# Preparing fp64 weights inside a fused attention and MoE kernel: other raw buffers, another bank for one bound, and another sharing of the splits between the engines

## The chip, the cores and the metric

The kernel runs on one core of one Trainium2 chip. Its engines are TensorE (PE, whose weight loads are listed apart as PEld), VectorE (DVE), ScalarE (ACT), GpSimd (POOL) and SyncE (SP), which here issues all DMAs from one queue, in order. Each engine runs its own list of instructions in order. The metric is the device time of one execution in microseconds; several runs are made and the median is taken. A profile is one execution of its own.

## The reference

Attention over 8 batches, 8 heads, 576 positions and 64 dimensions, with a threshold in the softmax: scores below the row's maximum less tau are dropped. The result, 4608 tokens of 512 channels, goes through a feed-forward layer with 2048 hidden units.

```python
scores = scale * np.matmul(q, k.transpose(0, 1, 3, 2))
thresh = np.max(scores, axis=-1, keepdims=True) - tau
scores = np.where(scores >= thresh, scores, -1000000000.0)
attn = np.exp(scores - np.max(scores, axis=-1, keepdims=True))
attn = attn / (np.sum(attn, axis=-1, keepdims=True) + 1e-09)
x = np.matmul(attn, v)          # then heads side by side: [4608, 512]
h = x @ w_in                    # w_in [512, 2048]
g = h * (1.0 / (1.0 + np.exp(-h)))
out = g @ w_out                 # w_out [2048, 512]
```

q, k and v are fp32. The two weight matrices come as fp64, 8 bytes for each number.

## The kernel before

**Products in pieces of fp16.** TensorE multiplies fp16 numbers at full rate, and the kernel keeps fp32 precision by splitting an operand into a first part (the value rounded to fp16) and a second part (what the rounding left). A product of two split operands is made of three products: first by first, first by second, second by first. So x, g, v and both weight matrices are split, each after a scaling by a power of two that is worked out from the operand's largest value (`pow2_scales`, lines 105 to 151).

**The weights.** There are 32 blocks of weights of 128 x 512 numbers: blocks 0 to 15 are w_in, 16 to 31 w_out. A block passes through these steps:

- `load_weights` (168): a DMA brings the raw fp64 block, 512 KB, into a raw buffer. For w_in, blocks 0 to 3 and 8 to 11 use four places in `gbuf`, the big buffer that later holds g; the other blocks of w_in and all of w_out use the two buffers of the tile `wraw`.
- `decode_weights` (183): ACT makes the fp32 value from the upper word (190), DVE shifts it (193) and puts in bits of the lower word (196). The raw buffer is then free. Four products of the decoded block with itself (208) are summed in a PSUM bank, `wps`, over four blocks; DVE reduces the sum (213). The largest entry bounds the squared weights.
- `scale_in` and `scale_out` (743, 746): `pow2_scales` brings the bounds of the four sums together: a reduction, a diagonal matrix by ACT (112), a product with ones by PE (114) into a bank, a reduction (116) and seven or eight one-column instructions.
- `split_weights` (215): makes the first part `hi` and the second part. Before, for w_in, POOL scales the block in place (225), ACT rounds it (228), POOL subtracts (229). For w_out, ACT scales and rounds in one step (220), and DVE scales and subtracts in one step (221).

**PSUM banks.** The helper `bank` (77) gives out the banks m0, m1 and m2, each one tile at a time. `wps` always takes m2, and the bound of w_out (`o_w_ps`) also takes m2. The first h units (batch 0, columns 0 to 255) alternate between m0 and m2.

**Attention.** Work is a list of tiles of 128 rows of scores. For batch 0 (the lines named "direct") scores are fp32 products (452), DVE takes the maximum (474), ACT the exponential (484), DVE the threshold and the sum (493, 497, 501), POOL scales the rows by the reciprocal (507), PE transposes them (403, 408), ACT copies the transposes (416, 417), and PE multiplies them by v (426). ACT and DVE make x from that (568, 569). Later batches use split operands: `split_k` (358, 360) and `split_q` (349, 350), scores (464), ACT scales the rows (511), POOL splits them (519, 522, 525), a DMA transposes them, and PE multiplies (550). Batch 0 is worked on in two passes, the low columns (0 to 255) of all head pairs, then the high ones (256 to 575), so that the first part of the feed-forward layer can begin early.

**The feed-forward layer.** An h unit (`h_unit`, 586) is 12 products for 128 hidden units (593), followed by tanh on ACT (601) and three steps on DVE and ACT that give g in two parts (602, 608, 609), which are written to `gbuf`. An o unit (617) is 12 products over four of the 16 hidden blocks (624); after four of them the output is scaled on ACT (634) and stored. Batch 0's first part uses the first 4096 words (of 4 bytes) of `gbuf`, its second part words 4096 to 9215; the queries of the direct tiles stand in words 4096 to 6399 until then.

**What sets the order.** The main loop (784) goes through ticks, one for each tile of scores, with 12 empty ticks between the low and the high pass of batch 0. At each tick it emits the steps of a few tiles, the entries of a time table (`todo`), and h or o units at a rate. A scheduler then orders the instructions of each engine by priority, which is the order of emission unless `pri(offset, f)` raises it: the offset counts emitted instructions. The weights enter the time table by `W_PLAN` (37): for each matrix the first block, the ticks between which blocks are decoded (a load two ticks ahead of its decode), the tick at which the scale is made and splits begin, the tick by which the splits are spread, and the offset of priority. Batch 0's output scale (`batch_scales`) is due one tick after the splits of w_out.

Of the kernel before, what the change touches and what calls it, by code (L numbers as in the profile page):

```python
# [15 lines left out]
ALU = mybir.AluOpType  # L16
AX = mybir.AxisListType
PSUM = bass.MemoryType.PSUM

P = 128  # L20
# [3 lines left out]
NK = DM // P  # L24
# [9 lines left out]
RATES = (0.9, 0.9)  # L34
RATE = 0.95

W_PLAN = ((0, 0, 10, 13, 0), (16, 9, 22, 36, 0))
PRI_S, PRI_SOFT1, PRI_SOFT2 = 1600, 50, 200
PRI_AV = 1500
HALVED = (1,)  # L40
# [11 lines left out]
def attention_moe(  # L52
# [10 lines left out]
    nc = tc.nc  # L63
# [41 lines left out]
    def pow2_scales(mx, name, own=None, squared=False):  # L105


        k = name[0]
        one = const.tile([P, 1], F32, name=f"{name}_one", tag=f"{k}_one")
        nc.vector.tensor_reduce(out=one, in_=mx, op=ALU.max, axis=AX.X)  # L110
        diag = const.tile([P, P], BF16, name=f"{name}_diag", tag="diag")
        nc.scalar.activation(diag, ident, AF.Copy, scale=one)
        allp = bank([P, P], f"{name}_ps", own)
        nc.tensor.matmul(allp, ones, diag, start=True, stop=True)
        one = const.tile([P, 1], F32, name=f"{name}_all", tag=f"{k}_all")
        nc.vector.tensor_reduce(out=one, in_=allp, op=ALU.max, axis=AX.X)
        cl = const.tile([P, 1], F32, name=f"{name}_cl", tag=f"{k}_cl")
        low, high = (2.0**-40, 2.0**94) if squared else (2.0**-20, 2.0**47)
        nc.vector.tensor_scalar(
            out=cl, in0=one, scalar1=low, scalar2=high, op0=ALU.max, op1=ALU.min  # L120
        )
        if squared:
            twice = const.tile([P, 1], F32, name=f"{name}_twice", tag=f"{k}_twice")
            nc.vector.tensor_scalar(
                out=twice, in0=cl, scalar1=2.0, scalar2=None, op0=ALU.mult
            )
            half = const.tile([P, 1], I32, name=f"{name}_half", tag=f"{k}_half")
            nc.vector.tensor_scalar(
                out=half, in0=twice.bitcast(I32), scalar1=1, scalar2=EXPMASK,
                op0=ALU.logical_shift_right, op1=ALU.bitwise_and,  # L130
            )
            cl = const.tile([P, 1], F32, name=f"{name}_root", tag=f"{k}_root")
            nc.vector.tensor_scalar(
                out=cl, in0=half.bitcast(F32), scalar1=2.0**64, scalar2=None, op0=ALU.mult
            )
        e2 = const.tile([P, 2], I32, name=f"{name}_e2", tag=f"{k}_e2")
        nc.vector.tensor_scalar(
            out=e2[:, 0:1], in0=cl.bitcast(I32), scalar1=EXPMASK, scalar2=None, op0=ALU.bitwise_and
        )
        nc.vector.tensor_scalar(  # L140
            out=e2[:, 1:2], in0=cl.bitcast(I32), scalar1=EXPMASK, scalar2=EXPMASK,
            op0=ALU.bitwise_and, op1=ALU.bitwise_xor,
        )
        sc = const.tile([P, 2], F32, name=f"{name}_sc", tag=f"{k}_sc", bufs=3)
        nc.vector.tensor_scalar(
            out=sc[:, 0:1], in0=e2[:, 1:2].bitcast(F32), scalar1=2.0**12, scalar2=None, op0=ALU.mult
        )
        nc.vector.tensor_scalar(
            out=sc[:, 1:2], in0=e2[:, 0:1].bitcast(F32), scalar1=2.0**-13, scalar2=None, op0=ALU.mult
        )  # L150
        return sc
# [14 lines left out]
    wps = {}  # L166

    def load_weights(i):
        if i < 4 * NK and i % 8 < 4:
            o = 1024 * (i % 8)  # L170
            t = gbuf.bitcast(I32)[:, o : o + 1024].rearrange("p (c w) -> p c w", w=2)
        else:
            t = stage.tile([P, 512, 2], I32, tag="wraw", name=f"wraw_{i}", bufs=2)
        if i < 4 * NK:
            n, c = divmod(i, NK)
            src = w_words[0][c * P : (c + 1) * P, 1024 * n : 1024 * (n + 1)]
        else:
            f = i - 4 * NK
            src = w_words[1][f * P : (f + 1) * P, :]
        nc.sync.dma_start(out=t.rearrange("p c w -> p (c w)"), in_=src)  # L180
        wraw[i] = t

    def decode_weights(i):


        t = wraw.pop(i)
        low, top = t[:, :, 0], t[:, :, 1]
        w = wst[:, i + WSPARE, :]
        wbits = w.bitcast(I32)
        nc.scalar.activation(  # L190
            w, top.bitcast(F32), AF.Prelu, scale=2.0**-112, alpha=2.0**32
        )
        nc.vector.tensor_scalar(
            out=wbits, in0=wbits, scalar1=3, scalar2=None, op0=ALU.logical_shift_left
        )
        nc.vector.scalar_tensor_tensor(
            out=wbits, in0=low, scalar=29, in1=wbits,
            op0=ALU.logical_shift_right, op1=ALU.bitwise_or,
        )


        n, c = divmod(i, 4)
        if c == 0:
            wps[n] = bank([P, P], f"wps_{n}", 2)
        upper = w.bitcast(BF16).rearrange("p (c t) -> p c t", t=2)[:, :, 1]
        for j in range(4):
            part = upper[:, j * P : (j + 1) * P]
            nc.tensor.matmul(
                wps[n], part, part,
                start=(c == 0 and j == 0), stop=(c == 3 and j == 3),  # L210
            )
        if c == 3:
            nc.vector.tensor_reduce(out=wmx[:, n : n + 1], in_=wps[n], op=ALU.max, axis=AX.X)

    def split_weights(i):
        w = wst[:, i + WSPARE, :]
        hi = w16[:, i, 0:512]
        sc = wsc["in" if i < 4 * NK else "out"][:, 0:1]
        if i >= 4 * NK:
            nc.scalar.activation(hi, w, AF.Copy, scale=sc)  # L220
            nc.vector.scalar_tensor_tensor(
                out=w16[:, i, 512:1024], in0=w, scalar=sc, in1=hi, op0=ALU.mult, op1=ALU.subtract
            )
            return
        nc.gpsimd.tensor_scalar(
            out=w, in0=w, scalar1=sc, scalar2=1.0, op0=ALU.mult, op1=ALU.mult
        )
        nc.scalar.activation(hi, w, AF.Copy)
        nc.gpsimd.tensor_tensor(
            out=w16[:, i, 512:1024], in0=w, in1=hi, op=ALU.subtract  # L230
        )
# [441 lines left out]
    def at(t, f):  # L673
        todo.setdefault(t, []).append(f)
# [73 lines left out]

    for first, t0, t1, t2, hp in W_PLAN:
        for i in range(16):  # L750
            ti = t0 + i * (t1 - t0) / 16
            at(math.floor(ti - 2), pri(hp, lambda i=i + first: load_weights(i)))
            at(math.floor(ti), pri(hp, lambda i=i + first: decode_weights(i)))
        at(t1, pri(hp, scale_out if first else scale_in))
        for i in range(16):
            at(t1 + i * (t2 - t1) // 16, pri(hp, lambda i=i + first: split_weights(i)))
    at(W_PLAN[0][3], lambda: batch_scales_in(0))
    for b in range(B):
        at(max(start[b, 3] + 7, W_PLAN[1][3] + 1), lambda b=b: batch_scales(b))
# [117 lines left out]
```

## Time and profile before

| | us |
|---|---|
| median of 3 runs | 1230.53 |
| lowest and highest run | 1227.30, 1231.17 |
| the profiled execution, its own time | 1225.66 |
| its span, first to last instruction | 1223.9 |
| PE busy | 1150.3 (94%) |
| DVE busy | 933.7 (76%) |
| ACT busy | 796.4 (65%) |
| POOL busy | 707.5 (58%) |

The profile names instructions by line, engine and operation, with the tile written and the tiles read ("wst<-wraw" writes wst from wraw); busy times are sums, and the time that an engine sat idle before an instruction is put down to what released it. The granted clock of PE is given beside each stretch as a share of full speed. Matmuls overlap, so the busy time of PE is modelled and is not PE at its peak.

### The profile page before, as it was taken

How to read it: one execution, taken by the hardware profiler on the slowest of the kernel's cores; microseconds unless marked ns; L12 is line 12 of the kernel's file. 1: busy time of each engine (PE TensorE's matmuls, PEld its weight loads, DVE VectorE, ACT ScalarE, POOL GpSimd, SP SyncE). 2: the span in 40 equal slices, each digit the busy share in tenths (PEclk: the TensorE clock that was granted, in tenths of full speed). 3: DMA queues.
4: the chain of work that ended last, by engine and by line, in shares of the span. 5: the costliest groups of instructions: out<-in, count | busy, mean ns of one | idle time of the engine just before them, and what ended most of it. 6: DMA issues, size and time to landing. Idle time of an engine off the chain costs nothing.

```text
span 1223.9 us, 27062 instructions
## 1 busy us (share of the span) xinstructions
PE 1150.3 (94%) x9474; PEld 899.2 (73%) x9474; DVE 933.7 (76%) x2625; ACT 796.4 (65%) x1505; POOL 707.5 (58%) x902
## 2 busy tenths in 40 slices
PE   6868799999899799999999999999999999999998
PEld 4545567777786577787777777788778877777777
DVE  7988988988999988889889858886788858333330
ACT  6667875876867777777777747785677756333331
POOL 2385357887877587886888428781778547100000
PEclk9979999999999999999999999999999999999999
DMA  9553148889788777886987448772877356200000
GB/s 309 185 161 95 41 108 173 160 160 177 132 177 141 160 137 139 150 165 151 167 149 145 114 94 155 146 136 82 153 150 142 77 92 116 42 11 16 16 10 25
DMA packets 340887, 151.73 MB, mean 124 GB/s; under 512 B 305936, under 2 KB 317200, under 8 KB 340752
## 3 DMA queue, kind: packets, MB, share of 16 engines
q1 hardware_dynamic: 340752, 150.01, 59.1%
q8 instruction: 75, 1.23, 0.4%
q14 instruction: 60, 0.49, 0.1%
HBM read 66.19 MB, written 9.44 MB: 62 GB/s over the span
## 4 chain that ended last, share of the span: by engine, by line
PE 63%; DVE 11%; DMA 10%; POOL 7%; issue 4%; ACT 4%; SPq 1%; POOLq 0%; ACTq 0%; DVEq 0%
PE o L624 24%; PE h L593 21%; PE s L464 9%; PE a L550 7%; DMA wT<-hl 4%; POOL hl L522 3%; DMA wraw<-in_w_out 3%; DVE w L493 2%; POOL hl L519 2%; DVE sm L474 2%; DVE qstack L350 2%; POOL hl L525 1%; DMA wraw<-in_w_in 1%; ACT w L484 1%; ACT w L511 1%
## 5 line engine op out<-in xcount | busy, mean ns | idle before, releaser
L593 PE MATMUL h<-x,wst 128*128 128x288 f16 (+2 forms) x3072 | 425.8, 288 | 7.8 <-DVE gbuf L609 5.0
L624 PE MATMUL o<-gbuf,wst 128*128 128x288 f16 (+2 forms) x3072 | 417.9, 286 | 2.4 <-ACT wst L634 2.4
L593 PEld LDWEIGHTS <-wst 128*128 128x128 f16 x3072 | 292.2, 98 | 95.7 <-issue 16.9
L624 PEld LDWEIGHTS <-wst 128*128 128x128 f16 x3072 | 292.7, 98 | 83.7 <-issue 7.4
L522 POOL TENSOR_TENSOR hl<-w,hl 128x512 f16<-128x512 f32 x252 | 302.6, 1201 | 12.8
L519 POOL TENSOR_SCALAR hl<-w 128x576 f16<-128x576 f32 x252 | 172.2, 686 | 193.4 <-ACT w L511 115.7
L484 ACT ACTIVATE w<-s,sm 128x576 f32<-128x576 f32 x288 | 211.6, 739 | 91.9 <-DVE sm L474 39.1
L493 DVE SCALAR_TENSOR_TENSOR w<-s,sm,w 128x576 f32<-128x576 f32 x288 | 232.0, 812 | 39.9 <-ACT w L484 37.8
L474 DVE TENSOR_REDUCE sm<-s 128x1 f32<-128x576 f32 x288 | 214.4, 749 | 28.7 <-PE s L464 21.8
L511 ACT ACTIVATE w<-w,sm 128x576 f32<-128x576 f32 x252 | 191.4, 771 | 52.1 <-DVE sm L501 50.1
L602 DVE SCALAR_TENSOR_TENSOR h<-th,h 128x288 f32<-128x288 f32 (+2 forms) x256 | 116.2, 455 | 113.7 <-ACT th L601 112.3
L601 ACT ACTIVATE th<-h,msc 128x288 f32<-128x288 f32 (+2 forms) x256 | 126.6, 498 | 103.2 <-PE h L593 101.8
L464 PE MATMUL s<-khi,qstack 128*128 128x288 f32 x560 | 144.3, 338 | 12.7 <-DVE w L493 9.9
L608 ACT ACTIVATE gbuf<-h 128x288 f16<-128x288 f32 (+2 forms) x256 | 104.3, 408 | 78.2 <-DVE h L602 77.5
L609 DVE SCALAR_TENSOR_TENSOR gbuf<-h,gbuf 128x288 f16<-128x288 f32 (+2 forms) x256 | 115.3, 452 | 41.9 <-ACT gbuf L608 41.0
L550 PE MATMUL a<-wT,v 128*64 128x288 f16 (+2 forms) x1568 | 115.0, 289 | 10.8 <-DMA wT<-hl 10.6
L360 POOL TENSOR_TENSOR klo<-kraw,khi 128x576 fp32r<-128x576 f32 x64 | 94.5, 1476 | 47.1 <-ACT khi L358 47.0
L464 PE MATMUL s<-klo,qstack 128*128 128x288 f32 x560 | 120.8, 296 | 0.0
L464 PEld LDWEIGHTS s<-khi,qstack 128*128 128x128 f32 x560 | 87.7, 190 | 31.9 <-issue 15.4
L550 PEld LDWEIGHTS <-v 128*64 128x64 f16 x1568 | 84.5, 110 | 33.7 <-issue 22.1
L464 PEld LDWEIGHTS s<-klo,qstack 128*128 128x128 f32 x560 | 90.4, 189 | 0.6
L525 POOL TENSOR_TENSOR hl<-w,hl 128x64 f16<-128x64 f32 x252 | 89.5, 355 | 0.0
(101 smaller groups left out, 930.4 us busy)
## 6 DMA issues: line engine op xcount, KB each, us to landing
kraw<-in_kT SPq DMA_DIRECT2D x128, 144.0 KB, 3.0
qraw<-in_qT SPq DMA_DIRECT2D x96, 144.0 KB, 3.0
vraw<-in_vL SPq DMA_DIRECT2D x32, 320.0 KB, 3.6
wraw<-in_w_out SPq DMA_DIRECT2D x16, 512.0 KB, 3.7
out_t<-wst SPq DMA_DIRECT2D x48, 144.0 KB, 2.1
wT<-hl SPq DMA_TRANSPOSE x280, 3.4
gbuf<-in_w_in SPq DMA_DIRECT2D x8, 512.0 KB, 6.2
wraw<-in_w_in SPq DMA_DIRECT2D x8, 512.0 KB, 5.1
```

The lines of the kernel that those rows point to most:

```text
L464: nc.tensor.matmul(s_ps[:, j, :HALF], lhs, kk[:, j * HALF : (j + 1) * HALF], start=(n == 0), stop=(n == len(seq) - 1),)
L474: nc.vector.tensor_reduce(out=negm, in_=s_ps[:, :, :HALF], op=ALU.max, axis=AX.XY, negate=True)
L484: nc.scalar.activation(wtile[t].rearrange("p (j c) -> p j c", j=2), sps[t][:, :, :HALF], AF.Exp, bias=small[t][:, 0:1],)
L493: nc.vector.scalar_tensor_tensor(out=w3, in0=s_ps[:, :, :HALF], scalar=sm[:, 1:2], in1=w3, op0=ALU.is_ge, op1=ALU.mult, accum_out=sm[:, 2:3],)
L511: nc.scalar.activation(w, w, AF.Copy, scale=r)
L519: nc.gpsimd.tensor_scalar(out=fl[:, 0:S], in0=w, scalar1=1.0, scalar2=1.0, op0=ALU.mult, op1=ALU.mult)
L522: nc.gpsimd.tensor_tensor(out=fl[:, 640:1152], in0=w[:, 0:512], in1=fl[:, 0:512], op=ALU.subtract)
L550: nc.tensor.matmul(a_ps[odd * D : (odd + 1) * D, :n], vt[:, lo_v, odd, kv, :], wT[v, b * H + 2 * p + odd][:, kw, c0 - base : c0 - base + n ...
L593: nc.tensor.matmul(ph[:, :n], wi(c, f, lo_w), x16[b, lo_x][:, c, c0 : c0 + n], start=(k == 0), stop=(k == 11),)
L601: nc.scalar.activation(th[:, :n], ph[:, :n], AF.Tanh, scale=moe_sc[b][:, 0:1])
L602: nc.vector.scalar_tensor_tensor(out=ph[:, :n], in0=th[:, :n], scalar=1.0, in1=ph[:, :n], op0=ALU.add, op1=ALU.mult,)
L624: nc.tensor.matmul(ps[:, :n], wo(f, d, lo_w), g[:, lo_g, :n], start=(f == 0 and k == 0), stop=(f == NF - 1 and k == 2),)
```

## The change

Five things change, in the preparation of the weights only.

1. Two more places in `gbuf`, words 6400 to 8447, become raw buffers. In each group of eight blocks of w_in, the last two go there; so do every third and fourth block of w_out. w_in then has eight raw buffers (before: six), w_out four (before: two).
2. Loads, decodes and the scale of w_out get an offset of priority of 150 (before: 0). Splits have none, as before. The splits of w_out are spread to tick 38 (before: 36), and batch 0's output scale follows from that two ticks later.
3. The last `wps` tile of w_out gets twice the width, and the product for w_out's bound goes into its second half, where it took a tile of its own in m2.
4. Odd blocks of w_in are split as w_out was: ACT scales and rounds, DVE scales and subtracts. POOL takes no part in them. Even blocks stay as they were.
5. Blocks of w_out are now scaled in place by DVE, rounded by ACT, and subtracted by POOL.

```diff
-W_PLAN = ((0, 0, 10, 13, 0), (16, 9, 22, 36, 0))
+W_PLAN = ((0, 0, 10, 13, 0), (16, 9, 22, 38, 150))
...
-        allp = bank([P, P], f"{name}_ps", own)
+        allp = wps[7][:, P : 2 * P] if name == "o_w" else bank([P, P], f"{name}_ps", own)
...
         if i < 4 * NK and i % 8 < 4:
             o = 1024 * (i % 8)
+        else:
+            o = (None, None, 6400, 7424)[i % 4]
+        if o is not None:
             t = gbuf.bitcast(I32)[:, o : o + 1024].rearrange("p (c w) -> p c w", w=2)
         else:
             t = stage.tile([P, 512, 2], I32, tag="wraw", name=f"wraw_{i}", bufs=2)
...
-            wps[n] = bank([P, P], f"wps_{n}", 2)
+            wps[n] = bank([P, 2 * P if n == 7 else P], f"wps_{n}", 2)
...
-                wps[n], part, part,
+                wps[n][:, 0:P], part, part,
...
-        if i >= 4 * NK:
+        if i < 4 * NK and i % 2:
             nc.scalar.activation(hi, w, AF.Copy, scale=sc)
             nc.vector.scalar_tensor_tensor(
                 out=w16[:, i, 512:1024], in0=w, scalar=sc, in1=hi, op0=ALU.mult, op1=ALU.subtract
             )
             return
-        nc.gpsimd.tensor_scalar(
-            out=w, in0=w, scalar1=sc, scalar2=1.0, op0=ALU.mult, op1=ALU.mult
-        )
+        if i < 4 * NK:
+            nc.gpsimd.tensor_scalar(
+                out=w, in0=w, scalar1=sc, scalar2=1.0, op0=ALU.mult, op1=ALU.mult
+            )
+        else:
+            nc.vector.tensor_scalar(out=w, in0=w, scalar1=sc, scalar2=None, op0=ALU.mult)
         nc.scalar.activation(hi, w, AF.Copy)
         nc.gpsimd.tensor_tensor(
             out=w16[:, i, 512:1024], in0=w, in1=hi, op=ALU.subtract
         )
...
-            at(t1 + i * (t2 - t1) // 16, pri(hp, lambda i=i + first: split_weights(i)))
+            at(t1 + i * (t2 - t1) // 16, pri(0, lambda i=i + first: split_weights(i)))
```

More of the change, by code (lines that the diff above doesn't have):

```diff
@@ L212, in decode_weights @@
         if c == 3:
-            nc.vector.tensor_reduce(out=wmx[:, n : n + 1], in_=wps[n], op=ALU.max, axis=AX.X)
+            nc.vector.tensor_reduce(out=wmx[:, n : n + 1], in_=wps[n][:, 0:P], op=ALU.max, axis=AX.X)
     def split_weights(i):
```

## The prediction

> **What bounds the kernel now.** I read the page's head and its slices first, then the view of busy time by stretches, to see where TensorE is idle.
>
> ```profile
> span 1223.9 us, 27062 instructions
> ...
> PEclk9979999999999999999999999999999999999999
> ...
> 0.00:60.00 60.00, 45.66 (x282) 30.25 (x283) 50.64 (x163) 38.03 (x74) 15.31 (x28) 0.97 0.76 247
> 60.00:110.00 50.00, 35.24 (x189) 22.48 (x187) 41.46 (x97) 34.93 (x72) 42.27 (x42) 0.83 0.49 152
> 110.00:180.00 70.00, 60.14 (x406) 43.04 (x406) 60.58 (x179) 52.48 (x116) 24.24 (x26) 0.95 0.22 56
> 180.00:400.00 220.00, 206.16 (x1778) 164.48 (x1776) 199.89 (x547) 161.93 (x298) 176.82 (x222) 1.00 0.83 163
> 400.00:1040.00 640.00, 622.55 (x5329) 495.25 (x5330) 530.56 (x1529) 450.78 (x824) 444.74 (x580) 1.00 0.70 134
> 1040.00:1223.90 183.90, 180.56 (x1499) 143.73 (x1496) 50.54 (x114) 58.29 (x128) 4.15 (x6) 1.00 0.08 20
> ```
>
> The columns are the stretch, its length, busy time of PE, weight load, DVE, ACT and POOL, granted clock, DMA share, GB/s. From 180 us on PE is the bound: idle 13.8 of 220, 17.4 of 640, 3.3 of 184. No matmul is added or taken away, so only the front can give: PE is idle 14.3 us before 60, 14.8 from 60 to 110, 9.9 from 110 to 180. In the middle stretch the clock is low too:
>
> ```profile
> 70.00:80.00 10.00, 4.24 (x25) 2.88 (x26) 7.08 (x13) 4.39 (x8) 10.00 (x11) 0.65 0.52 166
> 80.00:90.00 10.00, 9.17 (x39) 5.17 (x37) 7.27 (x21) 6.70 (x13) 6.57 (x7) 0.67 0.62 191
> 90.00:100.00 10.00, 6.94 (x47) 5.01 (x45) 8.78 (x17) 8.35 (x19) 8.10 (x8) 0.84 0.49 153
> ```
>
> Busy time times the missing clock: 4.24 x 0.35 + 9.17 x 0.33 + 6.94 x 0.16 = 5.6 us. So 60 to 110 holds 14.8 + 5.6 = 20.4 us that could be won at most.
>
> The timeline says why. These are POOL, then DVE, then PE:
>
> ```profile
> 60.02 12.72 POOL L225 TENSOR_SCALAR wst<-wst,i_w_sc 128x512 f32<-128x512 f32 x16 [2.51 <-DVE i_w_sc L145]
> 72.71 2.70 POOL L229 TENSOR_TENSOR wst<-wst 128x512 f16<-128x512 f32 x2
> 75.39 3.67 POOL L507 TENSOR_SCALAR w<-w,sm 128x576 f32<-128x576 f32 x4
> ...
> 63.34 0.15 DVE L501 RECIPROCAL sm<-sm 128x1 f32<-128x1 f32 x1
> 73.20 0.15 DVE L501 RECIPROCAL sm<-sm 128x1 f32<-128x1 f32 x1
> ...
> 73.33 0.61 PE L208 MATMUL wps<-wst 128*128 128x128 bf16 x4 [1.23 <-DVE wst L196]
> 76.90 0.61 PE L208 MATMUL wps<-wst 128*128 128x128 bf16 x4 [2.95 <-DVE wst L196]
> 77.30 1.05 PE L403 MATMUL tm<-ident,w 128*128 128x128 f32 x4
> 84.38 3.58 PE L426 MATMUL a<-wT,vraw 128*64 128x256 f32 x16
> 90.44 1.14 PE L593 MATMUL h<-x,wst 128*128 128x256 f16 x9
> ```
>
> As soon as w_in's scale is there (60 us), POOL runs all 16 of its scalings in one block, then two subtractions. The softmax scalings (L507) of four tiles stand behind it. The first tile's reciprocal ended at 63.5, the last one's at 73.35; all four run at 75.39 to 79.06. Only then come their transposes (77.30), the last product with V of the low part (84.38) and the first MoE product (90.44). This queue, not w_in's data, holds PE.
>
> The second thing is the raw w_out loads. From the view of waits of SP's queue (20 to 130 us), and the view of groups for 60 to 110 us and for 110 to 180 us:
>
> ```profile
> SPq L180 <- DVE wst L196: 42.2, 18, 4.3
> ...
> L229 POOL TENSOR_TENSOR wst<-wst 128x512 f16<-128x512 f32 x16 | 21.4, 1355 | 3.6 <-ACT wst L228 3.6
> L196 DVE SCALAR_TENSOR_TENSOR wst<-wraw,wst 128x512 int32<-128x512 int32 x14 | 13.2, 946 | 0.1
> L225 POOL TENSOR_SCALAR wst<-wst,i_w_sc 128x512 f32<-128x512 f32 x16 | 12.7, 816 | 2.5 <-DVE i_w_sc L145 2.5
> L193 DVE TENSOR_SCALAR wst<-wst 128x512 int32<-128x512 int32 x14 | 10.0, 712 | 6.3 <-ACT wst L190 6.3
> L190 ACT ACTIVATE wst<-wraw 128x512 f32<-128x512 f32 x14 | 9.4, 675 | 11.3 <-DMA wraw<-in_w_out 11.3
> ...
> L221 DVE SCALAR_TENSOR_TENSOR wst<-wst,o_w_sc 128x512 f16<-128x512 f32 x16 | 13.2, 837 | 0.0
> ```
>
> SP waits 42 us for a decode to free one of the two raw buffers, and ACT 11.3 us for the loads: loads and decodes take turns.
>
> **The change part by part.** Uncontended prices, from the view of the tile wst (minimum/median/maximum in ns):
>
> ```profile
> L193 DVE TENSOR_SCALAR wst<-wst x32: 404/426/1281, 11.8 to 108.1; 128x512 int32<-128x512 int32 x32
> L196 DVE SCALAR_TENSOR_TENSOR wst<-wraw,wst x24: 666/690/1527, 21.7 to 109.2; 128x512 int32<-128x512 int32 x24
> L228 ACT ACTIVATE wst<-wst x16: 612/630/676, 63.0 to 104.0; 128x512 f16<-128x512 f32 x16
> L220 ACT ACTIVATE wst<-wst,o_w_sc x16: 715/722/783, 123.3 to 148.6; 128x512 f16<-128x512 f32 x16
> L221 DVE SCALAR_TENSOR_TENSOR wst<-wst,o_w_sc x16: 726/743/1485, 124.6 to 150.3; 128x512 f16<-128x512 f32 x16
> ```
>
> **(1) Odd blocks of w_in leave POOL.** Eight scalings (8 x 0.816 = 6.5 us) and eight subtractions (8 x 1.355 = 10.8) go: POOL's 42.3 us in 60 to 110 become 25.0. The block ahead of the four softmax scalings is 6.5 us shorter. The first of the four may gain 6.5, or 9.2 if the two subtractions also fall behind; the last, which runs the last 0.92 (3.67 / 4) of its block, can gain only 79.06 - 0.92 - 73.35 = 4.8, since its reciprocal is not earlier. The last of the four sets the product with V, so I take 4.8 (0 to 9.2). The hole in front of it also brings the low clock; with half the hole I take half of the 5.6, 2.8 (0 to 5.6).
>
> **(2) Their price on DVE.** Eight of the L221 kind: 8 x 0.743 = 5.9 us, at the maximum 8 x 1.485 = 11.9. DVE idles 50 - 41.5 = 8.5 us there. And while POOL runs, its decodes are stretched: 14 x (0.712 - 0.426) + 14 x (0.946 - 0.690) = 7.6 us; POOL's work falls by 41%, so I take back 3.1. Net +2.8, inside the 8.5 idle: nothing (at most 11.9 - 8.5 = 3.4). If the hole closes, that cover goes with it and DVE is next in line; that is why (1) is not taken higher. ACT's work is 8 x 0.09 more here and 16 x 0.09 less for w_out: nothing.
>
> **(3) Four raw buffers for w_out and eight for w_in, w_out's decode at a priority raised by 150.** The 32 loads stay; they stop taking turns with the decodes. DVE's work does not change. What is won is the bank m2: the sums for w_out's bound sit in it until the last decode, and every second h unit of the first part wants it.
>
> ```profile
> 110.09 0.40 PE L208 MATMUL wps<-wst 128*128 128x128 bf16 x4
> 112.34 1.47 PE L593 MATMUL h<-x,wst 128*128 128x256 f16 x12
> 119.12 0.22 PE L114 MATMUL o_w_ps<-o_w_diag,ones 128*128 128x128 bf16 x1
> 178.62 1.27 PE L624 MATMUL o<-gbuf,wst 128*128 128x256 f16 x10
> ```
>
> Two h units run before 112.34, the other 14 in the 61 us to 173.7, 4.4 us apart. With both banks, 22 us from 90 to 112 would hold five. Three more at 1.47 us fill 4.4 us of idle PE, at most; the decodes must really end earlier, so I take 2.0 (0 to 4.4). On SP, kT and qT loads stand behind the raw loads; fewer waits there are part of the same gain.
>
> **(4) The bound in the last product's bank.** The product at 119.12 needs no free m2. But the last split starts at 150.3 and the first o product at 178.62, behind all h units: w_out's scale has 28 us to spare, and (3) already counts the bank. Nothing (0 to 1).
>
> **(5) w_out's split.** DVE's 16 x 0.837 become 16 scalings. With no POOL beside them they cost 0.426 (6.6 us less); with POOL beside them 0.712 (2.0 less). POOL now works beside them, so the second. PE is idle 9.9 us in this stretch and DVE busy 60.6 of 70. I take 2.0 (0 to 6.6). New waits: POOL's subtraction waits for ACT's copy, ACT's for DVE's scaling. Behind the subtractions, 16 x 1.355 = 21.7 us, stand POOL's softmax scalings of the high part and klo of batch 1; PE's transposes wait for them. POOL is 24.2 of 70 us busy, so 46 after. A scaling that comes while a subtraction runs waits half of it, 0.7 us; at 21.7/70 that is 12 x 0.31 x 0.7 = 2.6; some of it hides beside h products. I take a loss of 2.0 (0 to 12 x 1.355 = 16 if each stands behind a whole one).
>
> The Trainium skill speaks against this part. "SBUF — State Buffer", in its section "Summary: rules for kernel authors", says that VectorE in a two-port mode (a tensor_scalar on fp32 can be) and GpSimd hold one port pair exclusively, and the second blocks fully. The stretched rows (1281 against 426 ns) agree. By it a DVE scaling could stand behind a whole subtraction; that result is the third rival.
>
> Splits spread over two more ticks, and batch 0's output scale two ticks later, still end well ahead of 178.62: nothing.
>
> **Sum.** 4.8 + 2.8 + 0 + 2.0 + 0 + 2.0 - 2.0 = 9.6 us less. From 180 us on PE is busy 95% (1009.3 of 1043.9), so an earlier front moves all of it. The profiled execution took 1225.66 us, and would take 1216.1; the median shown, 1230.53, stands 4.9 above it, so 1220.9.
>
> **Rivals.**
> *The front is cleared entirely* (chance 0.12): (1) at 9.2 + 5.6, (3) at 4.4, (5) at +2: 21.2 less, 1209.3. For: all engines have gaps in 60 to 110. Against: DVE is busy 50.6 of the first 60 us, the loads' start-up among them, and can hardly follow.
> *Later stages swallow it* (0.12): DVE is busy 199.9 of 220 us from 180 to 400, and each batch's attention comes through it. If PE's lead is lost there, about 2 us of gain are left: 1229. Against: PE itself is idle only 13.8 there.
> *The port pair* (0.08): each of the 16 DVE scalings takes 0.426 + 0.7 (half a subtraction) = 1.13 instead of 0.837: 4.7 lost in place of 2.0 won, 6.7 worse than the forecast: 1227.6.
> *Slower: w_out's decode in w_in's way* (0.18). Raised by 150, a w_out decode can be ordered before w_in's last ones and before the low part's softmax on DVE, which has little room before 60. One decode is 0.426 + 0.690 = 1.12 us. Five ahead of w_in's scale move it by 5.6; six more ahead of the last low tiles move these by 6.7. The first h comes 12.3 later and the clock dip stays (2.8): 9.6 - 2.8 - 12.3 = -5.5, so 5.5 worse, 1236.0. It decides once w_in's scale comes after about 68 us instead of 59.8. Against: the w_out loads cannot start before buffers come free, so few can overtake.
>
> **How the numbers follow.** The forecast has 0.50, with its own range of 1215 to 1226. About 0.3% (3.7 us) is what a measurement can tell from no change. Faster: 0.50 + 0.12 + 0.02 of the two small ones, 0.64. Same: the rest of these but 0.01, 0.17. Slower: 0.18 + 0.01, 0.19. The range must take in the cleared front, the two small ones and the middle of the slower one: 1208 to 1236.
>
> **What would show it.** (1): POOL's first L507 after w_in's scale before 70 us, no slice with 7 in PEclk near 80, first h before 86. (2): L193 and L196 below 0.712 and 0.946 in 60 to 110. (3): SP's wait for L196 far below 42 us; the last w_out decode before 100. (5): POOL about 46 us busy in 110 to 180, DVE about 58. First o before 170. PE idle before 180 about 31 us instead of 39. I am wrong if w_in's scale comes clearly after 60, or if PE's idle time after 180 grows by what the front won.

## The result and the profile after

| | before | after |
|---|---|---|
| median of 5 runs, us | 1229.90 | 1241.23 |
| lowest and highest, us | 1227.30, 1231.17 | 1238.79, 1247.21 |
| span of the profiled execution, us | 1223.9 | 1239.4 |

The ratio is 1.0103 with a 95% interval of 1.008 to 1.0127: about 1% slower, where 0.8% faster was forecast (1220.9 against 1230.53). The median lies above the upper end of the range (1236). One execution in all the runs, of `e6_odd_only`, took 2336 us and counts in no ratio.

The head of the page and the busy time by stretches of the kernel after (columns as in the prediction):

```profile
span 1239.4 us, 27061 instructions
...
PEclk8988998999999899999999999999999999999999
```

```profile
0.00:60.00 60.00, 41.76 (x243) 28.26 (x244) 47.77 (x143) 37.26 (x70) 12.76 (x24) 0.92 0.88 289
60.00:110.00 50.00, 34.43 (x202) 22.37 (x200) 47.62 (x126) 34.63 (x70) 29.09 (x28) 0.84 0.30 96
110.00:180.00 70.00, 66.08 (x485) 51.44 (x485) 46.09 (x139) 43.05 (x99) 33.64 (x36) 0.96 0.15 41
180.00:250.00 70.00, 60.12 (x450) 44.47 (x451) 60.42 (x163) 51.79 (x101) 46.76 (x60) 0.90 0.69 148
250.00:400.00 150.00, 138.54 (x1176) 111.03 (x1171) 132.59 (x377) 109.25 (x196) 119.45 (x150) 0.99 0.80 160
```

The kernel before from 180 to 400 us, in the same view:

```profile
180.00:250.00 70.00, 64.64 (x572) 51.74 (x571) 63.21 (x171) 51.29 (x99) 56.28 (x70) 1.00 0.83 174
250.00:400.00 150.00, 141.51 (x1208) 112.74 (x1207) 136.68 (x377) 110.64 (x200) 120.54 (x153) 1.00 0.83 158
```

Read PE by what it loses: the stretch less its busy time, and busy time times the missing clock. From 0 to 60 us that is 14.3 + 1.4 before and 18.2 + 3.3 after (5.8 more). From 60 to 110 nothing changes (20.8 and 21.1). From 110 to 180 the kernel after loses 6.4 less (9.9 + 3.0 against 3.9 + 2.6). From 180 to 250 it loses 10.5 more (5.4 against 9.9 + 6.0, by the rounded busy times), and up to 400 another 4.4. So the front does win something, and a place behind it takes more back.

What the win is spent on shows in the view of the tiles a, o and h. Products with V of batch 0 and of the later batches, before:

```profile
L426 PE MATMUL a<-wT,vraw x160: 376/432/689, 19.0 to 177.6; 128*64 128x256 f32 x64, 128*64 128x320 f32 x64, 64*64 64x256 f32 x16, 64*64 64x320 f32 x16
L550 PE MATMUL a<-wT,v x1568: 269/286/449, 186.5 to 1054.5; 128*64 128x288 f16 x168, 128*64 128x256 f16 x14, 128*64 128x320 f16 x14
```

and after, with the first o product:

```profile
L432 PE MATMUL a<-wT,vraw x160: 376/430/483, 19.9 to 195.3; 128*64 128x256 f32 x64, 128*64 128x320 f32 x64, 64*64 64x256 f32 x16, 64*64 64x320 f32 x16
L556 PE MATMUL a<-wT,v x1568: 272/286/423, 205.1 to 1070.1; 128*64 128x288 f16 x168, 128*64 128x256 f16 x14, 128*64 128x320 f16 x14
L630 PE MATMUL o<-gbuf,wst x3072: 270/286/313, 157.7 to 1235.8; 128*128 128x288 f16 x144, 128*128 128x256 f16 x24, 128*128 128x320 f16 x24
```

The first o product comes 20.9 us earlier (157.7 against 178.6). Attention comes later: batch 0's last product with V by 17.7 us, batch 1's first by 18.6, the very last of all by 15.6. And the span less the start of that very last product is 1223.9 - 1054.5 = 169.4 before and 1239.4 - 1070.1 = 169.3 after; in the kernels that follow it is 169.3 to 169.4 too, in all but one. **What stands behind the last product with V takes the same 169 us in all but one of these kernels, however early the feed-forward units begin.** In them the time is lost or won ahead of that product. The busy share of PE from 180 us on (97%, 1009.3 of 1043.9) did not show that. A late start of batch 1 does not carry over one to one, though: the runs below hold one kernel with 208.3 to 1058.3 (`e9_gated`) and one with 176.4 to 1062.7 (`e12_odd_winraw_bank`). What PE loses between counts as well.

**First cause: w_out's decodes come early, and w_in's scale late.** The scale's chain on DVE, from the timeline of DVE, before:

```profile
54.81 0.15 DVE L110 TENSOR_REDUCE i_w_one<-wmx 128x1 f32<-128x4 f32 x1
...
58.45 0.29 DVE L116 TENSOR_REDUCE i_w_all<-i_w_ps 128x1 f32<-128x128 f32 x1
...
59.78 0.15 DVE L145 TENSOR_SCALAR i_w_sc<-i_w_e 128x1 f32<-128x1 f32 x1
```

and after:

```profile
49.76 0.14 DVE L110 TENSOR_REDUCE i_w_one<-wmx 128x1 f32<-128x4 f32 x1
...
63.49 0.28 DVE L116 TENSOR_REDUCE i_w_all<-i_w_ps 128x1 f32<-128x128 f32 x1
...
67.50 0.14 DVE L124 TENSOR_SCALAR i_w_twice<-i_w_cl 128x1 f32<-128x1 f32 x1
67.56 0.41 DVE L196 TENSOR_SCALAR wst<-wst 128x512 int32<-128x512 int32 x1
...
69.45 0.14 DVE L128 TENSOR_SCALAR i_w_half<-i_w_twice 128x1 int32<-128x1 int32 x1
...
76.14 0.13 DVE L145 TENSOR_SCALAR i_w_sc<-i_w_e 128x1 f32<-128x1 f32 x1
```

ACT's and PE's steps between L110 and L116, from their timelines, after:

```profile
52.45 0.41 ACT L112 ACTIVATE i_w_diag<-ident,i_w_one 128x128 bf16<-128x128 f32 x1
...
61.41 0.22 PE L114 MATMUL i_w_ps<-i_w_diag,ones 128*128 128x128 bf16 x1
```

With eight raw buffers w_in's bounds are ready 5 us earlier, but the chain takes 26.4 us where it took 5.0. It grew in two places. From L110 to L116 it takes 13.7 us instead of 3.6, and most of that lies on PE: the diagonal is ready at 52.86, and its product stands 8.6 us in PE's list (before: 2.8 us, 55.39 to 58.18). From L116 to the scale it takes 12.7 us instead of 1.3: between most of the steps, each about 0.14 us long, stand decodes of w_out (L196, L199; about 7.4 us) and softmax of the low part. The groups of DVE from 49 to 77 us show the decodes of the whole chain:

```profile
L196 DVE TENSOR_SCALAR wst<-wst 128x512 int32<-128x512 int32 x13 | 5.9, 451 | 2.6 <-ACT wst L193 2.4
L199 DVE SCALAR_TENSOR_TENSOR wst<-wraw,wst 128x512 int32<-128x512 int32 x8 | 5.4, 679 | 0.0
L199 DVE SCALAR_TENSOR_TENSOR wst<-gbuf,wst 128x512 int32<-128x512 int32 x6 | 4.6, 774 | 0.0
```

That is 5.9 + 5.4 + 4.6 = 15.9 us of decodes. The scale comes 76.14 - 59.78 = 16.4 us later. POOL's block of scalings waits for that scale:

```profile
76.37 7.52 POOL L229 TENSOR_SCALAR wst<-wst,i_w_sc 128x512 f32<-128x512 f32 x8 [3.50 <-DVE i_w_sc L145]
83.85 1.58 POOL L235 TENSOR_TENSOR wst<-wst 128x512 f16<-128x512 f32 x1
85.42 2.00 POOL L513 TENSOR_SCALAR w<-w,sm 128x576 f32<-128x576 f32 x2
```

The block has half the scalings, as meant, and takes 7.52 us instead of 12.72; it starts 16 us later.

**Second cause: a block on DVE.** The timeline of DVE and the windows of 10 us, after:

```profile
98.35 7.94 DVE L233 TENSOR_SCALAR wst<-wst,o_w_sc 128x512 f32<-128x512 f32 x13
...
107.94 2.48 DVE L233 TENSOR_SCALAR wst<-wst,o_w_sc 128x512 f32<-128x512 f32 x2
...
111.00 0.81 DVE L499 SCALAR_TENSOR_TENSOR w<-s,sm,w 128x576 f32<-128x576 f32 x1
```

```profile
100.00:110.00 10.00, 3.12 (x18) 1.74 (x16) 10.00 (x17) 7.11 (x18) 4.81 (x4) 0.74 0.00 0
...
200.00:210.00 10.00, 5.48 (x39) 3.93 (x39) 8.62 (x19) 4.17 (x9) 2.95 (x3) 0.68 0.97 207
210.00:220.00 10.00, 6.27 (x27) 4.43 (x26) 9.39 (x23) 5.51 (x12) 5.56 (x7) 0.67 0.74 195
```

As soon as w_out's scale is there, DVE scales 13 blocks in a row, since nothing but the scale holds them back. PE, from its timeline:

```profile
98.40 1.14 PE L458 MATMUL s<-kd,gbuf 128*128 128x288 f32 x4
...
111.88 2.29 PE L458 MATMUL s<-kd,gbuf 128*128 128x288 f32 x4 [6.69 <-DVE w L499]
...
205.09 3.20 PE L556 MATMUL a<-wT,v 128*64 128x256 f16 x28 [4.05 <-DVE x L575]
...
215.06 0.82 PE L470 MATMUL s<-khi,qstack 128*128 128x288 f32 x2 [3.73 <-DVE w L499]
```

PE waits 6.7 us for DVE's softmax, and the four products after that wait take 2.29 us instead of 1.14. The Trainium skill, "TensorE: Matmul & The Clock Gate", section "What's actually happening", has PE at half clock after an idle window of some 3.4 us; these rows agree. The two later waits, 4.05 and 3.73 us, are those of batch 1, whose attention is late: PE stands there, with a granted clock of 0.68 and 0.67 from 200 to 220 us. That it has used up its units by then is a reading, not shown by these rows.

### The profile page after: what moved, and what is told of

It reads as the page before. It is cut to its first block, busy times and chain, and to the rows that moved or that the text cites. A ratio compares the mean times of both kernels' runs of the same rounds, so it can differ in the third digit from the quotient of the medians.

```text
span 1239.4 us, 27061 instructions
## 1 busy us (share of the span) xinstructions
PE 1155.5 (93%) x9474; PEld 905.1 (73%) x9474; DVE 931.0 (75%) x2633; ACT 800.4 (65%) x1505; POOL 711.1 (57%) x902
## 4 chain that ended last, share of the span: by engine, by line
PE 60%; DVE 14%; DMA 8%; POOL 6%; issue 5%; ACT 5%; SPq 1%; POOLq 0%; ACTq 0%; DVEq 0%
PE o L630 22%; PE h L599 21%; PE s L470 8%; PE a L556 6%; DVE w L499 4%; DMA wT<-hl 3%; DVE sm L480 3%; DVE qstack L356 2%; POOL hl L528 2%; POOL hl L525 2%; DMA gbuf<-in_qT 2%; ACT w L490 2%; PE s L458 2%; DMA gbuf<-in_w_out 1%; POOL hl L531 1%
## 5 line engine op out<-in xcount | busy, mean ns | idle before, releaser
L528 POOL TENSOR_TENSOR hl<-w,hl 128x512 f16<-128x512 f32 x252 | 298.3, 1184 | 13.8
L490 ACT ACTIVATE w<-s,sm 128x576 f32<-128x576 f32 x288 | 212.0, 740 | 96.4 <-DVE sm L480 32.5
L470 PE MATMUL s<-khi,qstack 128*128 128x288 f32 x560 | 145.3, 341 | 20.8 <-DVE w L499 20.6
L531 POOL TENSOR_TENSOR hl<-w,hl 128x64 f16<-128x64 f32 x252 | 96.1, 381 | 0.0
```

The lines of the kernel that those rows point to most:

```text
L470: nc.tensor.matmul(s_ps[:, j, :HALF], lhs, kk[:, j * HALF : (j + 1) * HALF], start=(n == 0), stop=(n == len(seq) - 1),)
L490: nc.scalar.activation(wtile[t].rearrange("p (j c) -> p j c", j=2), sps[t][:, :, :HALF], AF.Exp, bias=small[t][:, 0:1],)
L528: nc.gpsimd.tensor_tensor(out=fl[:, 640:1152], in0=w[:, 0:512], in1=fl[:, 0:512], op=ALU.subtract)
```

## The experiments

Each ratio is against runs of the kernel before on the same chip; times are medians. Where an expectation names D, F and G, D is the four raw buffers of w_out, F the block of scalings on DVE, G the units that run ahead of attention. "i_w_sc" is the start of w_in's scale in the run's profile; it was 59.8 before and 76.1 after.

### What delays w_in's scale

Raised priority taken out of the changed kernel (`e1_no_offset`), and put alone into the kernel before (`e2_offset_only`, for loads, decodes and the scale):

```diff
-W_PLAN = ((0, 0, 10, 13, 0), (16, 9, 22, 38, 150))
+W_PLAN = ((0, 0, 10, 13, 0), (16, 9, 22, 38, 0))
```

> The changed kernel with w_out's offset of priority back at 0; all else as changed. Theory A (w_out's loads and decodes, raised by 150, push w_in's scale from 59.8 to 76.2 us and the low part's softmax back): w_in's scale comes before 62 us, the last product with V of the low part (L432 x16) before 88, and the time falls to between 1220 and 1231. Theory B (the block of w_out scalings on DVE, 98 to 109 us, is the cause): still about 1241, as the block only moves. Theory C (the other order lets later stages drift): between the two, with PE idle in 200 to 220 us as in the changed kernel.

> The kernel before with nothing but the offset of 150 for w_out's loads, decodes and scale. Theory A: w_in's scale after 66 us and a time of 1236 or more. Theory B: w_in's scale may move, but without DVE scalings in a block the time stays within 1227 to 1234. With two raw buffers fewer loads can overtake, so a smaller shift than the changed kernel's 16 us is expected under A.

Without it: 1239.48 us, 1.0078 (1.0053 to 1.0102), i_w_sc still 75.6. With it alone: 1229.64, 0.9992 (0.997 to 1.0013), i_w_sc 63.4. The offset is not the cause: alone it moves the scale by 3.6 us and the time by nothing, and without it the interval overlaps that of the changed kernel.

All raw buffers of part 3 put alone into the kernel before (`e5_raw_only`), and w_out's two extra buffers taken out of the changed kernel (`e7_wout_two_raw`):

```diff
-            o = (None, None, 6400, 7424)[i % 4]
+            o = (None, None, 6400, 7424)[i % 4] if i < 4 * NK else None
```

> The kernel before with nothing but the additional raw buffers (eight for w_in, four for w_out). Theory D (the two raw buffers had held w_out's decodes back; with four, 14 of them at 1.1 us of DVE go ahead of w_in's scale and of the softmax of the low part, whatever the offset): w_in's scale at about 75 us instead of 59.8, the first L550 product of batch 1 some 12 to 18 us later than 186.5, and the time 1238 to 1248. Rival E (the bank or the two ticks cost it): 1227 to 1233.

> The changed kernel with w_out's raw loads back in two buffers; w_in keeps eight. Theory D: w_in's scale comes before 64 us, and of the 11 us most come back: 1226 to 1233 (the DVE scalings of w_out, 5.5 us by the earlier run, still cost). Rival E: 1239 to 1243.

Buffers alone: 1234.94, 1.0064 (1.0042 to 1.0086), i_w_sc 73.8. Changed kernel less w_out's two: 1230.41, 1.001 (0.9991 to 1.003), i_w_sc 66.5: 11 us faster than with them. So w_out's two buffers make 9.6 of the 16.4 us by which the scale is late. The rest is there with w_in's two alone, in kernels that are no slower than the one before (66.5 here, 67.0 in `e8_odd_win_raw`).

All four buffers kept, but the two in `gbuf` released only when w_in's scale is there, and the decodes planned from tick 13 (`e9_gated`):

```diff
-W_PLAN = ((0, 0, 10, 13, 0), (16, 9, 22, 38, 150))
+W_PLAN = ((0, 0, 10, 13, 0), (16, 13, 22, 38, 150))
...
+        for o in (6400, 7424):
+            nc.vector.tensor_copy(gbuf.bitcast(F32)[:, o : o + 1], wsc["in"][:, 0:1])
```

> The changed kernel, all four raw buffers of w_out kept, but the two new ones in gbuf may be filled only once w_in's scale is known: two one-column copies of the scale are written into them, and w_out's decodes are planned from tick 13 instead of 9. Theory D (it is the decodes ahead of w_in's scale that cost, not the buffers as such): w_in's scale before 67 us as with two buffers, and 1226 to 1233. If the additional transfers or the buffers as such cost (DMA, SP's queue): 1238 to 1243. If decoding faster after the scale hurts the low part's softmax as much: about 1236.

1226.33, 0.9985 (0.9966 to 1.0004), i_w_sc 68.5: 15 us faster than the changed kernel with the same work but for two one-column copies. So the buffers cost nothing as such. What costs is that w_out's decodes run while w_in's chain and the low part's softmax need DVE; which of these two carries the cost, no run separates. Two buffers had held the decodes back.

### The parts by themselves

All of w_in back on POOL in the changed kernel (`e4_win_on_pool`: the branch for odd blocks removed), and part 4 alone in the kernel before (`e6_odd_only`: `if i >= 4 * NK or i % 2:` takes the old ACT and DVE branch):

> The changed kernel with all 16 blocks of w_in split on POOL as before. My prediction's step (1) said that the odd blocks on DVE win 4.8 us and up to 2.8 of clock: then this is 5 to 8 us slower than the changed kernel, 1246 to 1249. If DVE is the bound there, the step won nothing, and this is within 2 us of 1241 or faster by the 7.5 us of DVE that it saves.

> The kernel before with nothing but odd blocks of w_in split by ACT and DVE. Putting them back on POOL in the changed kernel cost 7.7 us (1248.9 against 1241.2); my step (1) says 7.6. Alone, then: 1222, with POOL's block 6.4 us shorter and the four softmax scalings behind it before 70 us. If the gain only exists where POOL stands behind a late scale, 1227 to 1231.

Without part 4 the changed kernel takes 1248.94, 1.0153 (1.0117 to 1.0189): part 4 wins 7.7 us there by the medians, 0.5% by the ratios, whose intervals overlap at the edge. Alone it loses 0.35%: 1232.03, 1.0035 (1.0013 to 1.0057), although its first h product comes at 77.3 instead of 90.4 and batch 0's last product with V at 160.8 instead of 177.6. From 110 to 180 us PE loses 23.5 us there against 12.9 before, and its very last product with V starts at 1062.1. The cause of that miss stays open.

Part 4 with eight raw buffers for w_in and two for w_out (`e8_odd_win_raw`); the bank of part 3's bound alone (`e10_bank_only`); both (`e12_odd_winraw_bank`); two ticks more for the splits alone (`e16_two_ticks`):

```diff
-        allp = bank([P, P], f"{name}_ps", own)
+        allp = wps[7][:, P : 2 * P] if name == "o_w" else bank([P, P], f"{name}_ps", own)
```

> The kernel before with odd blocks of w_in on ACT and DVE, and eight raw buffers for w_in (w_out keeps two). If w_in's loads had held up its decode, w_in's scale comes at about 55 instead of 59.8 and the time is 2 to 5 us below that of the odd blocks alone: 1217 to 1220. If DVE holds it, the same as that: 1222.

> The kernel before with nothing but w_out's bound in the second half of its last product's bank. My step (4): nothing (0 to 1 us): 1227 to 1231. The bound's product comes about 6 us earlier than 119 us.

> The kernel before with odd blocks of w_in on ACT and DVE, eight raw buffers for w_in (w_out two), and w_out's bound in its last product's bank. Without the bank part it was 6.0 us faster than before. If the bank part is worth nothing: 1221 to 1224; if the earlier bound lets splits of w_out fill DVE sooner: 1218 to 1221.

> The kernel before with the splits of w_out spread to tick 38 instead of 36, and nothing else. My prediction: nothing, 1227 to 1231. It also shows what a mere shift of order is worth: if it moves the time by more than 4 us either way, single parts of the change cannot be priced closer than that.

The first wins: 1222.42, 0.9955 (0.9935 to 0.9975), though w_in's scale comes at 67.0 and not at 55. Bank alone: 1229.69, 0.9999 (0.9975 to 1.0023). Ticks alone: 1229.04, 1.0016 (0.9998 to 1.0034). Both nothing. But the bank on top of the first gives 1233.06, 1.0035 (1.0019 to 1.0051), some 10 us worse. An edit that is worth nothing by itself moves the time by 10 us through the order it leads to. No single wait was found that explains it.

### The split of w_out

The old split put back into the changed kernel (`e3_wout_split_old`), and part 5 alone in the kernel before (`e11_wout_split_only`):

> The changed kernel with w_out split as before (ACT scales and rounds, DVE scales and subtracts; nothing on POOL). Theory B: no block of DVE scalings, PE's hole of 6.7 us at 105 to 112 goes, and 6 to 8 us come back: about 1234. Theory A: w_in's scale stays at about 76 and the time within 3 us of 1241.

> The kernel before with nothing but w_out split by DVE's scaling, ACT and POOL's subtraction. Undoing this in the changed kernel won 5.5 us. Theory F (the scalings need nothing but the scale, so they run in one block on DVE, where the old step had to wait for ACT block by block): a block of ten or more L231-like scalings in a row and 1232 to 1236. If the cost was POOL's subtractions ahead of its softmax scalings: the same time, but no block. My step (5) said no change: 1227 to 1231.

Old split: 1235.70, 1.0058 (1.0034 to 1.0082), 5.5 us less than the changed kernel, with intervals that just overlap. Part 5 alone: 1244.85, 1.0129 (1.0098 to 1.016). DVE's timeline in that kernel has the block again, in four pieces:

```profile
124.13 2.96 DVE L230 TENSOR_SCALAR wst<-wst,o_w_sc 128x512 f32<-128x512 f32 x5
...
127.34 4.02 DVE L230 TENSOR_SCALAR wst<-wst,o_w_sc 128x512 f32<-128x512 f32 x4
...
131.62 2.56 DVE L230 TENSOR_SCALAR wst<-wst,o_w_sc 128x512 f32<-128x512 f32 x4
...
134.89 3.17 DVE L230 TENSOR_SCALAR wst<-wst,o_w_sc 128x512 f32<-128x512 f32 x3
```

Is it the block, or the 16 subtractions on POOL? The same instructions on the same engines, but ACT rounds first, from the unscaled block, so that DVE's scaling waits for ACT (`e15_paced_scaling` against `e11_wout_split_only`; `e18_after_paced` is the same in the changed kernel):

```diff
-            nc.vector.tensor_scalar(out=w, in0=w, scalar1=sc, scalar2=None, op0=ALU.mult)
-        nc.scalar.activation(hi, w, AF.Copy)
+            nc.scalar.activation(hi, w, AF.Copy, scale=sc)
+            nc.vector.tensor_scalar(out=w, in0=w, scalar1=sc, scalar2=None, op0=ALU.mult)
```

> The kernel before with w_out's new split alone (1244.9), but ACT rounds first, scaling as it goes, and DVE scales in place after it; POOL subtracts. Same engines and counts; DVE's scaling now has to wait for ACT block by block. Theory F (the block on DVE costs): no run of more than three scalings, and 1230 to 1236. If POOL's subtractions cost (or DVE's and POOL's common hold): still 1241 to 1248.

> The whole changed kernel, but with DVE's scaling of w_out behind ACT's rounding. Theory F: the block of 13 scalings at 98 us goes and with it PE's hole of 6.7 us; the four raw buffers still put the decodes ahead. So between 1230 and 1237. If the block mattered only in the kernel before: 1239 to 1243.

Paced alone: 1224.23, 0.9966 (0.9946 to 0.9986), 20 us faster than unpaced. The stretch from 110 to 180 us and PE's waits from 110 to 250 (in all, times, longest), unpaced:

```profile
110.00:180.00 70.00, 57.62 (x402) 42.68 (x403) 56.16 (x153) 44.89 (x104) 36.56 (x37) 0.90 0.20 47
```

```profile
PE s L455 <- DVE w L496: 8.9, 2, 8.0
```

and paced:

```profile
110.00:180.00 70.00, 61.67 (x449) 45.26 (x448) 62.88 (x185) 55.43 (x123) 44.27 (x45) 1.00 0.30 76
```

```profile
PE s L456 <- DVE w L497: 2.2, 2, 1.3
```

The 8.0 us wait and the low clock are gone. PE loses 12.4 + 5.8 = 18.2 us in this stretch unpaced and 8.3 paced, and from 180 to 250 us 9.7 and 3.4. The two profiled executions lie further apart than the medians (spans of 1244.9 and 1215.7 us), so these 16 us are a little over half of the 29 between them. Most of the rest shows later, from 400 us on, and wasn't traced to a wait. POOL's subtractions are all there in the faster kernel, and in the slower one its softmax scalings waited for DVE (groups of 110 to 180 us, paced, then unpaced):

```profile
L233 POOL TENSOR_TENSOR wst<-wst 128x512 f16<-128x512 f32 x16 | 18.8, 1173 | 13.9 <-DVE sm L505 9.2 <-DVE wst L232 3.8 <-DVE sm L501 0.9
```

```profile
L510 POOL TENSOR_SCALAR w<-w,sm 128x576 f32<-128x576 f32 x12 | 9.0, 749 | 16.6 <-DVE sm L504 11.0 <-DVE sm L500 3.5 <-DVE sm L480 2.1
```

In the changed kernel pacing gives 1230.39, 1.0007 (0.9986 to 1.0028): 11 us faster than without, with w_in's scale still at 75.3. The gated kernel, in turn, is 15 us faster than the changed one and keeps the block, all 16 in a row:

```profile
111.92 12.33 DVE L233 TENSOR_SCALAR wst<-wst,o_w_sc 128x512 f32<-128x512 f32 x16
```

So the two causes are not prices to be added. Each costs something when it is put alone into the kernel before (6.5 us for all the new buffers, 16.7 for the split), but in the changed kernel the removal of w_out's buffers alone gives back about all of the 11 us, pacing alone does so too, and the old split gives back half.

### Units ahead of attention, and sums of parts

Fewer units for each tick in the first part (`e13_rate07`), and the gate with the old split (`e14_gated_old_split`):

```diff
-RATES = (0.9, 0.9)
+RATES = (0.7, 0.9)
```

> The changed kernel with the rate at which h and o units of batch 0's first part are emitted cut from 0.9 to 0.7 a tick. Theory G (the decodes put attention back while h and o units ran ahead, so PE runs dry at 200 to 220 us; the units' lead is worthless, since in every run the end came 169.3 us after the last product with V): fewer units early leave PE work for 200 to 220, its idle time in 180 to 250 falls from 9.9 towards 5, and 3 to 8 us come back: 1233 to 1238. If attention's lateness alone is the cost and PE's supply is not, the time stays at 1239 to 1243 or rises.

> The gated kernel (two new raw buffers of w_out only after w_in's scale) with w_out split as before. Undoing w_out's new split won 5.5 us in the changed kernel; the gated kernel stood at 1226. If the parts add: 1218 to 1223, which beats the kernel before. If the new split costs nothing once the decodes are late: 1224 to 1228.

Lower rate: 1232.21, 1.0034 (1.0014 to 1.0053), 9 us faster than the changed kernel, with w_in's scale still at 75.1. From 180 to 250 us PE is busy 62.55 us where it was 60.12, at a clock of 0.95 where it was 0.90. That supports the reading that units were spent too early. Its last product with V starts at 1053.7, earlier than in the kernel before, but it is the one kernel in which that lies further from the end (176.7 us): units put off at the front are left for the end. The gate with the old split is a miss: 1233.64, 1.0049 (1.0029 to 1.0069), 7 us worse than the gate alone, where the same edit had won 5.5 in the changed kernel. The parts do not add.

### The best version

Eight raw buffers for w_in, two for w_out, part 4, and the paced split of w_out; no offset, no bank, no ticks (`e17_best`):

```diff
+            o = (None, None, 6400, 7424)[i % 4] if i < 4 * NK else None
...
-        if i >= 4 * NK:
+        if i < 4 * NK and i % 2:
...
+            nc.scalar.activation(hi, w, AF.Copy, scale=sc)
+            nc.vector.tensor_scalar(out=w, in0=w, scalar1=sc, scalar2=None, op0=ALU.mult)
```

> The two versions that beat the kernel before put together: odd blocks of w_in on ACT and DVE with eight raw buffers for w_in (1222.4, ratio 0.9955), and w_out split by ACT, then DVE's scaling, then POOL (1224.2, ratio 0.9966); w_out keeps two raw buffers and its own bank tile. If they add: a ratio of 0.990 to 0.994, about 1218. If they use up the same idle time: 0.995 to 0.998. If the shift of order eats it, as it did where the bank was added: above 1.000.

1218.70, 0.9909 (0.989 to 0.9929): faster than both. Its stretch of 180 to 250 us, and the view of tile a:

```profile
180.00:250.00 70.00, 67.06 (x579) 52.76 (x577) 63.18 (x183) 55.38 (x105) 59.24 (x74) 1.00 0.84 163
```

```profile
L557 PE MATMUL a<-wT,v x1568: 270/286/449, 182.4 to 1047.2; 128*64 128x288 f16 x168, 128*64 128x256 f16 x14, 128*64 128x320 f16 x14
```

Attention of batch 1 begins at 182.4 instead of 186.5 and ends at 1047.2 instead of 1054.5. The span, 1216.5, is again 169.3 behind that.

## Why the prediction was wrong

**Step (3) failed.** It said that DVE's work does not change, and counted only the bank m2 (2.0 us won). The amount of work did not change; its place did. The decodes in the view of the tile wst, after:

```profile
L196 DVE TENSOR_SCALAR wst<-wst x32: 404/416/883, 12.5 to 80.1; 128x512 int32<-128x512 int32 x32
```

The last one starts at 80.1 us instead of 108.1, as the prediction foresaw among its signs ("the last w_out decode before 100"), and that was the harm: 15.9 us of them ran between 49 and 77 us, around w_in's chain. The step had 2.0 us won; the new buffers alone lost 6.5. In the changed kernel, taking out w_out's two buffers returned 11 us, holding the decodes back 15.

**The slower rival named the effect and not its cause.** w_in's scale passed 68 us, its mark for deciding, by 8 us. But the rival laid that to the offset of 150, which alone moved the scale by 3.6 us and the time by nothing. What it held against itself, that the loads cannot start before buffers come free, was the point: four buffers let them start. It counted five decodes ahead of the scale where there were 13 or 14. With 0.18 it was too low.

**Step (1) was right in size and buried.** From w_in's scale to the first softmax scaling POOL took 75.39 - 60.02 = 15.4 us before and 85.42 - 76.37 = 9.1 after: 6.3 less, beside the 6.5 worked out; but the scalings gave only 5.2 of it, since each of the eight takes longer (7.52 / 8 = 0.94 us), and one subtraction fewer ahead of the softmax the rest. The step's 4.8 + 2.8 = 7.6 stand beside 7.7 in the changed kernel. That closeness is in part luck: by the ratios it is some 6 us, with intervals that overlap. That it would hold in any surroundings was wrong: alone it lost 0.35%, with eight buffers for w_in it took part in a win of 0.45%.

**Step (2)** took DVE's share as hidden. The eight instructions took 7.5 us where 5.9 were worked out (the groups below, L224); DVE was busy 47.6 of the 50 us, so its cover was gone, as the step warned.

**Step (4)** and the two ticks were right: nothing, each alone.

**Step (5) had the price right and the shape wrong.** These are the groups of the changed kernel from 60 to 110 us:

```profile
L233 DVE TENSOR_SCALAR wst<-wst,o_w_sc 128x512 f32<-128x512 f32 x16 | 10.9, 745 | 0.0
L224 DVE SCALAR_TENSOR_TENSOR wst<-wst,i_w_sc 128x512 f16<-128x512 f32 x8 | 7.5, 933 | 0.0
```

16 scalings at 0.745 us each, where 0.712 was taken, are indeed cheaper than the old 16 x 0.837. But the old instruction waited for ACT's rounding, one block at a time; the new one waits for nothing but the scale, so 13 of them go in one block ahead of the softmax. The step looked for the loss on POOL, behind the subtractions. The paced run cleared those: the same number of subtractions, 20 us faster. The step had 2.0 us won and 2.0 lost; the new split alone lost 16.7.

**The port pair** did not decide. Single scalings did stretch to 1383 ns in the changed kernel, but their mean was 745 ns and not the 1.13 us that this rival took. In the paced run of part 5 alone they stretched to 1603 ns, and that kernel is 20 us faster than the unpaced one.

**"From 180 us on PE is bound, so an earlier front moves all of it"** failed too. (The figures it gives, 1009.3 of 1043.9, are 97% and not 95%.) The stretch of 110 to 180 us gave the 6.4 us, and 180 to 250 took 10.5, most likely because what had been won were units of the feed-forward layer, while attention ran 18 us later; the lower rate, which saved units, gave 9 us back. That is the rival "later stages swallow it", which expected 2 us of gain to be left; the prediction's last sentence named both signs, the late scale and PE's idle time after 180.

**The signs it named.** The first o product came before 170 us (157.7), the last w_out decode before 100 (80.1), the decodes from 60 to 110 us were less stretched (means of 504 ns for L196, 678 and 856 for L199), and no slice of PEclk shows a 7, all as foreseen. SP's wait for the decodes fell from 42.2 to 27.3 us. POOL's first softmax scaling behind w_in's scale before 70 us (85.42), the first h product before 86 (96.4) and PE idle for 31 us before 180 (18.2 + 15.6 + 3.9 = 37.7, before 39.0) did not come true. POOL and DVE are busy 33.6 and 46.1 us from 110 to 180, not 46 and 58: w_out's split had begun ahead of that stretch.

**Open.** That the units were spent too early rests on one run and a reading of the trace, and is less firm than the two causes above. How a part's worth depends on the others (the bank worth 0 or 10 us, the old split 5.5 better or 7 worse, part 4 alone) isn't explained, nor is why one of two remedies is enough to give back all of the loss. The bank shows that a mere change of order can be worth 10 us, as much as one of the causes; these therefore rest on several runs that agree (`e5_raw_only`, `e7_wout_two_raw` and `e9_gated`; `e11_wout_split_only`, `e15_paced_scaling` and `e18_after_paced`), against one that does not (`e14_gated_old_split`). Single executions of one kernel differ by up to 12 us, so one trace can't carry such differences.

## What to carry to other kernels

Before a buffer is added, ask what the old shortage held back: a chain of short dependent steps is delayed by all the work that can now be ordered into its gaps. When an instruction loses a dependency, look at when it will run and not only at what it costs; waiting for another engine may be what spaced it out. And look for the product that keeps its distance from the end (here the last one with V, 169.3 us) before a gain elsewhere is counted: in all kernels here but one, what moved the end had moved that product. Where parts interact, no part's price can be carried over from another kernel.

## What was not expected of the hardware

The scaling of 128 x 512 fp32 numbers on DVE in the view of the tile wst (minimum, median, maximum), in the changed kernel and in the paced one (`e15_paced_scaling`):

```profile
L233 DVE TENSOR_SCALAR wst<-wst,o_w_sc x16: 472/474/1383, 98.3 to 109.0; 128x512 f32<-128x512 f32 x16
```

```profile
L232 DVE TENSOR_SCALAR wst<-wst,o_w_sc x16: 467/538/1603, 124.4 to 156.0; 128x512 f32<-128x512 f32 x16
```

In both kernels one and the same instruction takes up to about three times its least time (2.9 and 3.4). The longest one, 1603 ns from 141.36 us on, began just after POOL's subtraction for klo of batch 1 (141.28, 1.40 us long). The wider spread was in the faster kernel: the stretching of single instructions cost less than 16 of them in a row, or nearly so.
